# Attention keys in chunks of 128, 128, 128 and 64 in place of four chunks of 112

## The chip, the cores and the metric

The program runs on one core of a Trainium2 chip. The metric is the device time of one execution in microseconds (us); lower is better. Beside the timed runs one execution was recorded by the hardware profiler, and all lines of a profile below are from such an execution.

## What is computed

An attention block over 8 batches of 12 heads, with 448 positions and 64 values per head, followed by a two-layer block. All data is float32, only the two weight matrices arrive as float64.

```python
# q, k, v: (8, 12, 448, 64)
rmsnorm(x, g) = x / sqrt(mean(x * x, axis=-1) + 1e-6) * g
scores = (1 / 8) * rmsnorm(q, g_q) @ rmsnorm(k, g_k).T
attn   = exp(scores - max) / (sum(exp(scores - max)) + 1e-9)
o      = attn @ v                      # (8, 12, 448, 64)
x      = o.transpose(0, 2, 1, 3).reshape(3584, 768)
h      = x @ w_in                      # (3584, 2048)
out    = (h - tanh(h)) @ w_out         # (3584, 768)
```

## The kernel before

The work is cut into 48 steps: 8 batches times 6 pairs of heads. A step `s` has these parts, each a function that the diff touches:

- `load` fetches q, k and v of the pair. A tile holds 112 partitions with 4 positions each (`CP` = 112, `NCH` = 4): position 4p+c is chunk c of partition p. q and v come in one DMA each, k in one per head. All go through the queue of SyncE (SP), which also carries the weights (`weight_load`, `ring_load`) and the output (`store`), in the order in which the program writes them.
- `squares` (ScalarE) and `norm` (VectorE, then GpSimd for the power -0.5) give the reciprocal root mean squares `rr`; `norm_q` scales q by them. k is not scaled: its factor enters as the scale of the exponential.
- `turn` transposes the four chunks of k and of q on TensorE and copies them out as `kT` and `qT`: the two heads lie on rows 0 to 63 and 64 to 127, the 448 positions on columns.
- `scores(s, half)`: for two of the four chunks of keys, and for both heads, one product of 64 rows (the head's values) by 112 columns (the chunk's keys) with all 448 queries moving. Two such products, one per head, stand on the two row halves of TensorE. ScalarE then takes the exponential into `p`, keys on partitions.
- `add` (VectorE, from step 10 on) sums the four chunks of `p` into `sum`, `totals` multiplies that sum (or, before step 10, the four chunks themselves) by ones, 32 columns wide, four products side by side on column quarters, and takes the reciprocal `rs`.
- `values`: for each chunk four products of 112 rows by 32 columns with 448 queries moving, side by side on the four column quarters of TensorE, accumulated over the chunks in one bank of PSUM. `divide` multiplies by `rs` into `xT`; GpSimd builds three combinations from those (`tt`).

The two layers of the second block are done batch by batch with a seven-product scheme on half matrices (`products`: 128 x 128 weights, 224 columns moving, tile names `mm<-xT,w_f`, `mm<-gT,w_f`, `mm<-tt,w_f`, `mm<-tg,w_f`, line L510). From batch 1 on their weights are fetched through a ring of six slots, five products ahead. In batch 0 they are built on the way from the float64 words by ScalarE, VectorE and GpSimd.

The order of instructions is written out by hand. `first_slot` runs for steps -3 to 5, while there is nothing of the second block to do. `slot(s)` runs for steps 6 to 47: it places the parts of steps s to s+4 around four calls of `run(gap)`, each of which puts a fixed share of the second block's products of the batch before on TensorE. What is left of them at the end follows in `run(1e9)`. TensorE takes its instructions in this order, so a part that becomes cheaper there brings all that follows forward.

PSUM has eight banks: five are handed out in turn by `sc_bank`, three by `mm_bank`. Who takes a bank waits until its last user's reader is done.

Every float32 product is two instructions of TensorE (two passes), each a weight load (PEld) and a matmul (PE).

Of the kernel before, what the change touches and what calls it, by code (L numbers as in the profile page):

```python
# [91 lines left out]

def bounded_path(tc, ctx, q, k, v, moe_w_in, moe_w_out, out, g_col, ident, ones, neg_half):

# [33 lines left out]
    BL = 32  # L128
    assert HS * 2 == S and HC * 2 == CD and SETS * 4 == CF and HC * P == HALF and S % BL == 0

# [23 lines left out]
    def load(s, names):  # L154
        b, hp = steps[s]
        for name in names:
            src = {"q": q, "k": k, "v": v}[name]
            bufs = 3 if name == "v" else 2
            pair = src[b, 2 * hp : 2 * hp + 2].rearrange("h (p c) d -> p h c d", c=NCH)
            if name == "k":  # L160
                t = nat.tile([CP, NCH, 2, D], F32, name="k_nat", bufs=bufs)
                for h in range(2):
                    nc.sync.dma_start(out=t[:, :, h, :], in_=pair[:, h])
            else:
                t = nat.tile([CP, 2, NCH, D], F32, name=f"{name}_nat", bufs=bufs)
                nc.sync.dma_start(
                    out=t.rearrange("p h c d -> p h (c d)"), in_=pair.rearrange("p h c d -> p h (c d)")
                )
            loaded[name, s] = t
# [174 lines left out]
    def squares(s):  # L344
        n = nat.tile([CP, NCH, 2, D], F32, name="n", bufs=1)
        sq = nat.tile([CP, 2 * NCH, D], F32, name="sq", bufs=1), n.rearrange("p c h d -> p (c h) d")
        normed[s] = sq, n
        for i, name in ((1, "q"), (0, "k")):
            nc.scalar.activation(sq[i], loaded[name, s].rearrange("p a b d -> p (a b) d"), AF.Square)

    def norm(s):

        sq, n = normed[s]
        rr = small.tile([CP, 2, 2 * NCH], F32, name="rr", bufs=3)
        for group in ((1,), (0,)) if s < NP else ((0, 1),):
            for i in group:
                nc.vector.reduce_sum(rr[:, i], sq[i], axis=AX.X)  # L357
            r = rr[:, group[0] : group[-1] + 1].rearrange("p i r -> p (i r)")
            nc.vector.tensor_scalar(out=r, in0=r, scalar1=1.0 / D, scalar2=1e-6, op0=ALU.mult, op1=ALU.add)  # L359
            nc.gpsimd.tensor_tensor(out=r, in0=r, in1=neg_half[:, : r.shape[1]], op=ALU.pow)  # L360
        normed[s] = rr, n

    def norm_q(s):
        rr, n = normed[s]
        t = loaded.pop(("q", s))
        nc.vector.tensor_tensor(  # L366
            out=n.rearrange("p c h d -> p h c d"), in0=t,
            in1=rr[:, 1].rearrange("p (h c) -> p h c", h=2)[:, :, :, None].to_broadcast([CP, 2, NCH, D]),
            op=ALU.mult,
        )  # L370

    def turn(s, tk, tq):

        rr, n = normed.pop(s)
        kn = loaded.pop(("k", s))
        for c in range(NCH):
            nc.tensor.transpose(tk[:, c * CP : (c + 1) * CP], kn[:, c].rearrange("p h d -> p (h d)"), ident[:CP, :CP])  # L377
        kT = qkp.tile([P, S], F32, name="kT")
        nc.scalar.mul(kT, tk[:, :S], g_col)
        for c in range(NCH):  # L380
            nc.tensor.transpose(  # L381
                tq[:, c * CP : (c + 1) * CP], n[:, c].rearrange("p h d -> p (h d)"), ident[:CP, :CP]
            )
        qT = qkp.tile([P, S], F32, name="qT")
        nc.scalar.copy(out=qT, in_=tq[:, :S])
        turned[s] = rr, kT, qT
# [3 lines left out]

    def scores(s, half):

        rr, kT, qT = turned[s]
        p = probs[s, half] = pp.tile([CP, 2, NCH // 2, S], F32, name="p")
        for i in range(NCH // 2):
            c = half * (NCH // 2) + i
            tiles = []
            for h in range(2):
                r = slice(h * D, (h + 1) * D)
                sc = sc_bank()  # L400
                nc.tensor.matmul(  # L401
                    sc[:CP, :S], lhsT=kT[r, c * CP : (c + 1) * CP], rhs=qT[r, :], start=True, stop=True
                )
                tiles.append(sc)
            for h in range(2):
                nc.scalar.activation(  # L406
                    p[:, h, i, :], tiles[h][:CP, :S], AF.Exp, scale=rr[:, 0, 2 * c + h : 2 * c + h + 1]
                )

    def add(s):  # L410

        if s <= NP + NP // 2:
            sums[s] = []
            return
        t = sp.tile([CP, 2, S], F32, name="sum")
        sums[s] = [t]
        parts = [probs[s, c // 2][:, :, c % 2, :] for c in range(NCH)]
        nc.vector.tensor_tensor(out=t, in0=parts[0], in1=parts[1], op=ALU.add)  # L418
        for part in parts[2:]:
            nc.vector.tensor_tensor(out=t, in0=t, in1=part, op=ALU.add)  # L420

    def values(s, av):
        v_nat = loaded.pop(("v", s))
        for c in range(NCH):
            p = probs[s, c // 2]
            for m in range(2):
                for h in range(2):
                    r = (2 * m + h) * BL
                    nc.tensor.matmul(  # L429
                        av[r : r + BL, :S], lhsT=v_nat[:, h, c, m * BL : (m + 1) * BL], rhs=p[:, h, c % 2, :],  # L430
                        start=(c == 0), stop=(c == NCH - 1),
                    )
        return av

    def totals(s, dn):

        t = sums.pop(s)
        parts = t if t else [probs[s, c // 2][:, :, c % 2, :] for c in range(NCH)]
        for i, p in enumerate(parts):
            for n in range(2):  # L440
                for h in range(2):
                    r = (2 * n + h) * BL
                    nc.tensor.matmul(  # L443
                        dn[r : r + BL, :HS], lhsT=ones[:CP, :BL], rhs=p[:, h, n * HS : (n + 1) * HS],
                        start=(i == 0), stop=(i == len(parts) - 1),
                    )
# [3 lines left out]
    def divide(s, av):  # L450
# [3 lines left out]
        for n in range(2):  # L454
            for m in range(2):
                nc.vector.tensor_tensor(  # L456
                    out=x[m * D : (m + 1) * D, n * HS : (n + 1) * HS],
                    in0=av[m * D : (m + 1) * D, n * HS : (n + 1) * HS], in1=rs[n * D : (n + 1) * D], op=ALU.mult,
                )
        del probs[s, 0], probs[s, 1]  # L460
        if hp < HC:
# [257 lines left out]
    def first_slot(s):  # L719

        if has(s + 1):
            scores(s + 1, 0)
        if has(s + 2):
            turn(s + 2, mm_bank(), sc_bank())
        if s > -3:
            load(s + 4, "kq")
        squares(s + 3)
# [5 lines left out]
        if has(s + 1):  # L733
            scores(s + 1, 1)
            add(s + 1)
        av = values(s, mm_bank()) if has(s) else None
        norm_q(s + 3)
# [5 lines left out]
    def slot(s):  # L743
# [3 lines left out]
        if has(s + 1):  # L747
            scores(s + 1, 0)
        if has(s + 2):
            load(s + 2, "v")  # L750
# [5 lines left out]
        if has(s + 4):  # L756
            load(s + 4, "kq")
        run(gap)
        if s >= 2 * NP:
            totals(s, sc_bank())  # L760
        divide(s, values(s, sc_bank()))
        if has(s + 1):
            scores(s + 1, 1)
            add(s + 1)
# [6 lines left out]

    load(0, "kq")
    load(1, "kq")
    weight_load(0)
# [11 lines left out]
def general_path(tc, ctx, q, k, v, moe_w_in, moe_w_out, out, g_col, ident, neg_half):  # L786
# [67 lines left out]
    def prep(s):  # L854

        for name in ("k", "q"):
# [9 lines left out]
            )  # L866
            nc.gpsimd.tensor_tensor(out=rr, in0=rr, in1=neg_half[:, : 2 * NCH], op=ALU.pow)
            nc.vector.tensor_tensor(
# [145 lines left out]
def kernel(  # L1014
# [22 lines left out]
    consts = ctx.enter_context(tc.tile_pool(name="consts", bufs=1))  # L1037
    grow = consts.tile([1, 2, D], F32, name="grow")
    nc.scalar.dma_start(out=grow[:, 0, :], in_=g_q[None, :])
    nc.scalar.dma_start(out=grow[:, 1, :], in_=g_k[None, :])  # L1040
    gcol = consts.tile([P, 2], F32, name="gcol")
    for base in (0, D):
        nc.scalar.dma_start(out=gcol[base : base + D, 0:1], in_=g_q[:, None])
        nc.scalar.dma_start(out=gcol[base : base + D, 1:2], in_=g_k[:, None])
    prod = consts.tile([1, D], F32, name="prod")
    nc.vector.tensor_tensor(out=prod, in0=grow[:, 0, :], in1=grow[:, 1, :], op=ALU.mult)
    nc.vector.tensor_tensor(out=prod, in0=prod, in1=prod, op=ALU.mult)
    most = consts.tile([1, 1], F32, name="most")
    nc.vector.tensor_reduce(out=most, in_=prod, op=ALU.max, axis=AX.X)
    flag = consts.tile([1, 1], I32, name="flag")  # L1050
    nc.vector.tensor_scalar(
# [9 lines left out]
    nc.vector.memset(ones, 1.0)  # L1061
    neg_half = consts.tile([CP, 4 * NCH], F32, name="neg_half")
    nc.vector.memset(neg_half, -0.5)
    bounded = nc.values_load(flag[0:1, 0:1])

    with tc.If(bounded) as cmp:
        with ExitStack() as arm, tc.manual_schedule():
            bounded_path(tc, arm, q, k, v, moe_w_in, moe_w_out, out, g_col, ident, ones, neg_half)
    with cmp.Else():
# [32 lines left out]
```

## Time and profile before

| | |
|---|---|
| time of four runs | 1471.97 to 1474.83 us, median 1474.04 us |
| the profiled execution | 1471.86 us; span of its instructions 1470.1 us; granted TensorE clock 0.996 |
| busy, share of the span | PE 98%, PEld 78%, VectorE (DVE) 55%, ScalarE (ACT) 32%, GpSimd (POOL) 35% |
| DMA engines, mean share | 57.6% for the queue with all data |
| PE busy, 0 to 80 us | 60.75 us of 80 |
| PE busy, 330 to 1330 us | 999.26 us of 1000 |

How to read the lines: a group has the code line, the engine, the operation, the names of output and inputs, the tile's shape (rows*columns of weights, then partitions x elements that move), the count, the busy time and the mean nanoseconds of one, and behind the bar the time that the engine stood idle before them. In a timeline the first number is the start in us from the span's start, the second how long the merged row lasts; a row of PE ends with the drain of its last matmul, so the start of the next row tells the pace better than the length does. `xN` is the number of merged instructions, and in brackets stands the idle time before the row.

### The profile page before, as it was taken

The page shows a single profiled execution, that of the slowest core. Times are in us where ns is not written, and L with a number is a line of the kernel's source. Part 1 is how long each engine was busy: PE and PEld are TensorE (multiplying, and loading weights), DVE is VectorE, ACT ScalarE, POOL GpSimd, SP SyncE. Part 2 cuts the span into 40 slices and gives each one's busy share as a digit, 9 for nine tenths or more (in the row PEclk, how much of TensorE's full clock was granted, in tenths as well). Part 3 has the DMA queues.
Part 4 walks back from the last instruction along what each step waited for, and adds up shares of the span by engine and source line. Part 5 has one row for each costly group of instructions (what it writes and reads, how often), then busy time and mean ns, then how long its engine had stood idle before and what let it go on. Part 6 is the DMA issues. An engine that isn't in the chain of part 4 may idle for free.

```text
span 1470.1 us, 22159 instructions
## 1 busy us (share of the span) xinstructions
PE 1437.3 (98%) x8544; PEld 1146.7 (78%) x8544; DVE 806.7 (55%) x1162; ACT 468.4 (32%) x850; POOL 510.2 (35%) x336
## 2 busy tenths in 40 slices
PE   6889999999999999999999999999999999999997
PEld 2357744578887888788878887888788878889997
DVE  3889987756434653456445554545554366433322
ACT  6755544223222332133322332223322233201100
POOL 4556565233421343224423233322342134312310
PEclk9999999999999999999999999999999999999999
DMA  9759788954465454644454545555545654455563
GB/s 184 154 156 235 247 241 221 261 181 138 135 182 172 139 184 130 184 140 153 155 181 135 167 135 185 146 137 170 167 148 142 182 162 138 146 163 158 186 191 98
DMA packets 244998, 247.33 MB, mean 168 GB/s; under 512 B 143380, under 2 KB 187156, under 8 KB 244884
## 3 DMA queue, kind: packets, MB, share of 16 engines
q1 hardware_dynamic: 244560, 245.82, 57.6%
q8 instruction: 70, 1.15, 0.3%
q14 instruction: 44, 0.36, 0.1%
q10 hardware_dynamic: 324, 0.00, 0.0%
HBM read 212.34 MB, written 33.42 MB: 167 GB/s over the span
## 4 chain that ended last, share of the span: by engine, by line
PE 88%; DVE 7%; DMA 2%; issue 1%; SPq 1%; ACT 1%; POOL 1%; ACTq 0%; DVEq 0%; POOLq 0%
PE mm L510 62%; PE sc L401 9%; PE sc L429 8%; PE mm L675 4%; PE sc L443 2%; PE sc L381 1%; DMA q_nat<-in_q_dram 1%; PE sc L377 1%; DVE rr L357 1%; DVE sum L420 1%; DVE xT L456 1%; DMA w_raw<-in_moe_w_out_dram 1%; PE mm L429 1%; DVE w_out L275 1%; DVE sum L418 0%
## 5 line engine op out<-in xcount | busy, mean ns | idle before, releaser
L406 ACT ACTIVATE p<-sc,rr 112x448 f32<-112x448 f32 x384 | 212.2, 638 | 466.6 <-PE sc L401 454.6
L510 PE MATMUL mm<-xT,w_f 128*128 128x224 f32 x1392 | 279.4, 355 | 0.9 <-DVE s L576 0.6
L510 PEld LDWEIGHTS mm<-xT,w_f 128*128 128x128 f32 x1392 | 259.8, 190 | 20.3 <-issue 11.3
L510 PEld LDWEIGHTS mm<-gT,w_f 128*128 128x128 f32 x1344 | 251.4, 190 | 23.4 <-issue 22.7
L510 PE MATMUL mm<-gT,w_f 128*128 128x224 f32 x1344 | 267.7, 355 | 0.0
L360 POOL TENSOR_TENSOR rr<-rr,neg_half 112x16 f32<-112x16 f32 (+1 forms) x54 | 146.2, 2711 | 318.2 <-DVE rr L359 311.4
L510 PE MATMUL mm<-tt,w_f 128*128 128x224 f32 x1044 | 211.2, 354 | 0.0
L510 PEld LDWEIGHTS mm<-tt,w_f 128*128 128x128 f32 x1044 | 196.1, 190 | 8.0 <-issue 8.0
L510 PE MATMUL mm<-tg,w_f 128*128 128x224 f32 x1008 | 200.4, 353 | 0.0
L510 PEld LDWEIGHTS mm<-tg,w_f 128*128 128x128 f32 x1008 | 189.5, 190 | 0.0
L401 PE MATMUL sc<-qT,kT 64*112 64x448 f32 x768 | 175.3, 570 | 1.8 <-ACT p L406 1.2
L547 POOL TENSOR_TENSOR gT<-s,th 128x448 f32<-128x448 f32 x96 | 119.5, 1254 | 150.1 <-ACT th L546 149.5
L470 POOL TENSOR_TENSOR tt<-xT,tt 128x224 f32<-128x224 f32 x23 | 32.5, 1412 | 346.7 <-DVE xT L456 346.7
L401 PEld LDWEIGHTS sc<-qT,kT 64*112 64x112 f32 x768 | 63.5, 176 | 92.0 <-issue 78.9
L429 PE MATMUL sc<-p,v_nat 112*32 112x448 f32 x1344 | 134.1, 539 | 0.0
L420 DVE TENSOR_TENSOR sum<-sum,p 112x896 f32<-112x896 f32 x76 | 93.9, 1235 | 7.9
L429 PEld LDWEIGHTS sc<-p,v_nat 112*32 112x32 f32 x1344 | 43.1, 110 | 69.0 <-issue 64.1
L456 DVE TENSOR_TENSOR xT<-sc,rs 64x224 f32<-64x224 f32 x168 | 65.2, 388 | 57.7 <-PE sc L429 53.9
L546 ACT ACTIVATE th<-s 128x448 f32<-128x448 f32 x96 | 55.2, 578 | 119.0 <-DVE s L576 67.5
L366 DVE TENSOR_TENSOR n<-q_nat,rr 112x512 f32<-112x512 f32 x48 | 53.3, 1110 | 69.8 <-POOL rr L360 69.8
L448 DVE RECIPROCAL rs<-sc 128x224 f32<-128x224 f32 x42 | 65.4, 1558 | 39.4 <-PE sc L443 39.3
L629 DVE TENSOR_TENSOR s<-mm,s 128x224 f32<-128x224 f32 x21 | 8.2, 392 | 131.8 <-PE mm L510 131.8
(97 smaller groups left out, 1384.1 us busy)
## 6 DMA issues: line engine op xcount, KB each, us to landing
w_f<-w_in SPq DMA_DIRECT2D x196, 384.0 KB, 3.7
w_f<-w_out SPq DMA_DIRECT2D x147, 512.0 KB, 4.3
w_raw<-in_moe_w_out_dram SPq DMA_DIRECT2D x16, 768.0 KB, 5.3
k_nat<-in_k_dram SPq DMA_DIRECT2D x96, 112.0 KB, 3.5
q_nat<-in_q_dram SPq DMA_DIRECT2D x48, 224.0 KB, 4.4
v_nat<-in_v_dram SPq DMA_DIRECT2D x48, 224.0 KB, 4.6
out_dram<-th SPq DMA_DIRECT2D x192, 56.0 KB, 1.9
w_in<-w_out SPq DMA_DIRECT2D x21, 384.0 KB, 6.8
```

The lines of the kernel that those rows point to most:

```text
L360: nc.gpsimd.tensor_tensor(out=r, in0=r, in1=neg_half[:, : r.shape[1]], op=ALU.pow)
L366: nc.vector.tensor_tensor(out=n.rearrange("p c h d -> p h c d"), in0=t, in1=rr[:, 1].rearrange("p (h c) -> p h c", h=2)[:, :, :, None].to_ ...
L401: nc.tensor.matmul(sc[:CP, :S], lhsT=kT[r, c * CP : (c + 1) * CP], rhs=qT[r, :], start=True, stop=True)
L406: nc.scalar.activation(p[:, h, i, :], tiles[h][:CP, :S], AF.Exp, scale=rr[:, 0, 2 * c + h : 2 * c + h + 1])
L420: nc.vector.tensor_tensor(out=t, in0=t, in1=part, op=ALU.add)
L429: nc.tensor.matmul(av[r : r + BL, :S], lhsT=v_nat[:, h, c, m * BL : (m + 1) * BL], rhs=p[:, h, c % 2, :], start=(c == 0), stop=(c == NCH - 1),
L448: nc.vector.reciprocal(rs, dn[:, :HS])
L456: nc.vector.tensor_tensor(out=x[m * D : (m + 1) * D, n * HS : (n + 1) * HS], in0=av[m * D : (m + 1) * D, n * HS : (n + 1) * HS], in1=rs[n ...
L510: nc.tensor.matmul(bank[:, f * HS : (f + 1) * HS], lhsT=w[:, c * width + f, :], rhs=moving[p](c), start=(first and f == 0 and c == 0), sto ...
L546: nc.scalar.activation(th, h, AF.Tanh, bias=0.0, scale=1.0)
L547: eng.tensor_tensor(out=g[:, rows, cols], in0=h, in1=th, op=ALU.subtract)
L675: nc.tensor.matmul(bank[:, :S], lhsT=w_out_row(f, n // HC)[:, n % HC * P : (n % HC + 1) * P], rhs=g[:, f, :], start=(f == 0), stop=(f == C ...
```

## The change

The keys of a step go in three chunks of 128 and one of 64. A chunk of 128 holds positions 3p+c of the first 384; the last one holds positions 384 to 447. k and v of the last chunk are loaded twice, onto partitions 0 to 63 and 64 to 127, so k and v take two more DMAs each per step. q is issued ahead of k.

`turn` transposes k with 128 rows, so the last chunk's 64 keys come out twice; 448 of the 512 columns are copied. `scores` is called per chunk. For the chunks of 128 a product is 64 rows by 128 columns with 448 queries; for the last chunk there are four products of 64 rows by 64 columns with 224 queries each, on the four quarters of TensorE: row half by head, column half by half of the queries. So `p` of the last chunk has the first 224 queries on partitions 0 to 63 and the others on 64 to 127.

`values` works on 224 queries at a time in two banks. The last chunk goes first, in `last_values`: eight products of 64 rows by 32 columns with 224 queries, two row halves by four column quarters. Then follow, for each half of the queries, three chunks of 128 rows by 32 columns.

In `slot` the order of one turn changes: chunks 0 and 1 at its start (as before); behind the second `run(gap)` the last chunk's scores of step s+1, the last chunk's values of step s, the totals, the other values, and then the scores of chunk 2 (before: totals, values, scores of chunks 2 and 3). `norm` treats q and k apart in every step (before: in the first six alone), so there are two smaller powers on GpSimd in place of one.

```diff
@@ load
-            pair = src[b, 2 * hp : 2 * hp + 2].rearrange("h (p c) d -> p h c d", c=NCH)
-            if name == "k":
-                t = nat.tile([CP, NCH, 2, D], F32, name="k_nat", bufs=bufs)
-                for h in range(2):
-                    nc.sync.dma_start(out=t[:, :, h, :], in_=pair[:, h])
...
+                full, rest = pair[:, :K0].rearrange("h (p c) d -> h p c d", c=KF), pair[:, K0:]
+                if name == "v":
+                    t = nat.tile([P, 2, NCH, D], F32, name="v_nat", bufs=bufs)
+                    last = t[:, :, KF]
+                    nc.sync.dma_start(
+                        out=t[:, :, :KF].rearrange("p h c d -> p h (c d)"), in_=full.rearrange("h p c d -> p h (c d)")
+                    )
+                else:
+                    t = nat.tile([P, NCH, 2, D], F32, name="k_nat", bufs=bufs)
+                    last = t[:, KF]
+                    for h in range(2):
+                        nc.sync.dma_start(out=t[:, :KF, h], in_=full[h])
+                for r in range(2):
+                    nc.sync.dma_start(out=last[r * KR : (r + 1) * KR], in_=rest.rearrange("h p d -> p h d"))
@@ norm
-        for group in ((1,), (0,)) if s < NP else ((0, 1),):
...
+        for i, rows in ((1, CP), (0, P)):
+            r = rr[:rows, i]
+            nc.vector.reduce_sum(r, sq[i], axis=AX.X)
@@ turn
-            nc.tensor.transpose(tk[:, c * CP : (c + 1) * CP], kn[:, c].rearrange("p h d -> p (h d)"), ident[:CP, :CP])
+            nc.tensor.transpose(tk[:, c * P : (c + 1) * P], kn[:, c].rearrange("p h d -> p (h d)"), ident)
@@ scores
+        halves, keys, n = (1, P, S) if c < KF else (2, KR, HS)
+        name, bufs = ("p", 2) if c < 2 else ("p_full", 1) if c < KF else ("p_last", 2)
...
+        for i in range(halves):
             for h in range(2):
                 r = slice(h * D, (h + 1) * D)
                 nc.tensor.matmul(
-                    sc[:CP, :S], lhsT=kT[r, c * CP : (c + 1) * CP], rhs=qT[r, :], start=True, stop=True
+                    tiles[h][i * keys : (i + 1) * keys, :n], lhsT=kT[r, c * P : c * P + keys],
+                    rhs=qT[r, i * n : (i + 1) * n], start=True, stop=True,
                 )
@@ add
+        nc.vector.tensor_tensor(out=t, in0=p[0], in1=p[1], op=ALU.add)
+        nc.vector.tensor_tensor(out=t, in0=t, in1=p[2], op=ALU.add)
+        for n in range(2):
+            part = t[n * KR : (n + 1) * KR, :, n * HS : (n + 1) * HS]
+            nc.vector.tensor_tensor(out=part, in0=part, in1=last[n * KR : (n + 1) * KR], op=ALU.add)
@@ new function
+    def last_values(s, av):
+        v_nat, p = loaded["v", s], probs[s, KF]
+        for n in range(2):
+            keys = slice(n * KR, (n + 1) * KR)
+            for m in range(2):
+                for h in range(2):
+                    r = (2 * m + h) * BL
+                    nc.tensor.matmul(
+                        av[n][r : r + BL, :HS], lhsT=v_nat[keys, h, KF, m * BL : (m + 1) * BL],
+                        rhs=p[keys, h, 0], start=True, stop=False,
+                    )
@@ values
-        for c in range(NCH):
...
-                        av[r : r + BL, :S], lhsT=v_nat[:, h, c, m * BL : (m + 1) * BL], rhs=p[:, h, c % 2, :],
-                        start=(c == 0), stop=(c == NCH - 1),
+        for n in range(2):
+            for c in range(KF):
...
+                            av[n][r : r + BL, :HS], lhsT=v_nat[:, h, c, m * BL : (m + 1) * BL],
+                            rhs=p[c][:, h, n * HS : (n + 1) * HS], start=False, stop=(c == KF - 1),
@@ first_slot
-            load(s + 4, "kq")
+            load(s + 4, "qk")
...
-            scores(s + 1, 1)
+            scores(s + 1, KF)
+        if has(s):
+            av = [mm_bank() for _ in range(2)]
+            last_values(s, av)
+            values(s, av)
+        if has(s + 1):
+            scores(s + 1, 2)
             add(s + 1)
-        av = values(s, mm_bank()) if has(s) else None
@@ slot
+        if has(s + 1):
+            scores(s + 1, KF)
+        dn = sc_bank() if s >= 2 * NP else None
+        av = [sc_bank() for _ in range(2)]
+        last_values(s, av)
         if s >= 2 * NP:
-            totals(s, sc_bank())
-        divide(s, values(s, sc_bank()))
+            totals(s, dn)
+        divide(s, values(s, av))
         if has(s + 1):
-            scores(s + 1, 1)
+            scores(s + 1, 2)
             add(s + 1)
```

Before step 10 `totals` takes the last chunk with `half_ones`, ones on one half of the partitions and zeros on the other, so it still issues sixteen products. `divide` reads the two banks. The pools for `p` hold as much as before.

## The prediction

> **What bounds the kernel now.** I read the busy shares first, then the windows, then one turn of `slot` in the timeline.
>
> ```profile
> PE 1437.3 (98%) x8544; PEld 1146.7 (78%) x8544; DVE 806.7 (55%) x1162; ACT 468.4 (32%) x850; POOL 510.2 (35%) x336
> 0.00:80.00 80.00, 60.75 (x484) 26.41 (x484) 51.04 (x85) 55.22 (x97) 40.47 (x29) 0.98 0.85 176
> 330.00:1330.00 1000.00, 999.26 (x5998) 826.89 (x5991) 512.31 (x744) 285.79 (x541) 319.33 (x217) 1.00 0.52 155
> ```
>
> From about 120 us on, TensorE has no gaps: 999.26 us of 1000 in the long window, with VectorE at 51% and the DMA engines at 0.52. A microsecond less of TensorE work in `slot` is a microsecond less of time, unless something new makes it wait. Only the first 80 us (`first_slot`) are different. A busy row does not say how fast TensorE goes, so the starts in one turn come next (PE, then the weight loads):
>
> ```profile
> 825.22 0.35 PE L510 MATMUL mm<-xT,w_f 128*128 128x224 f32 x1
> 825.51 0.59 PE L443 MATMUL sc<-sum,ones 112*32 112x224 f32 x8
> 825.91 3.19 PE L429 MATMUL sc<-p,v_nat 112*32 112x448 f32 x32
> 829.03 1.76 PE L401 MATMUL sc<-qT,kT 64*112 64x448 f32 x8
> 830.72 0.46 PE L510 MATMUL mm<-xT,w_f 128*128 128x224 f32 x1
> ...
> 826.29 0.13 PEld L429 LDWEIGHTS sc<-p,v_nat 112*32 112x32 f32 x4 [0.25 <-issue]
> 826.66 0.13 PEld L429 LDWEIGHTS sc<-p,v_nat 112*32 112x32 f32 x4 [0.25 <-issue]
> ...
> 829.03 0.27 PEld L401 LDWEIGHTS sc<-qT,kT 64*112 64x112 f32 x4 [0.73 <-issue]
> 829.50 0.18 PEld L401 LDWEIGHTS sc<-qT,kT 64*112 64x112 f32 x2 [0.20 <-issue]
> 829.87 0.18 PEld L401 LDWEIGHTS sc<-qT,kT 64*112 64x112 f32 x2 [0.20 <-issue]
> 830.72 0.30 PEld L510 LDWEIGHTS mm<-xT,w_f 128*128 128x128 f32 x2 [0.67 <-issue]
> ```
>
> Weight loads come in fours (`values`) or twos (`scores`), and a group of 448 columns advances every 0.376 us (826.29, 826.66), whether it holds four products or two. `values` is 8 such groups, 825.91 to 829.03 = 3.12 us; half a step's scores are 4 groups, 829.03 to 830.72 = 1.69 us. What goes beyond 8 x 0.376 = 3.01 and 4 x 0.376 = 1.50 is the price of changing the tile's shape. It has two parts. The last group lasts longer: the last values group starts near 828.54, the scores 0.49 later, 0.11 too long; from the last scores group (830.25) to L510 it is 0.47, 0.10 too long; L510's own passes are 0.19 apart, and from its last (825.22) to the totals it is 0.29, 0.10 too long. And the first group's weights are not loaded ahead: 0.47 to the second scores group, 0.09 too long with 112 columns of weights; 0.30 to L510's second pass, 0.11 too long with 128; 0.02 too long for the totals' 32 (their second pass starts at 825.72). So a change of shape costs 0.12 us into 32 columns, 0.18 to 0.20 into the scores and 0.20 into L510.
>
> **The change part by part**, for one turn of `slot`.
>
> *Work removed.* Scores: 8 groups of 448 become 6 of 448 and 2 of 224 (four quarters at once, two passes). A group of 224 advances every 0.19 (totals, below), so 3.01 becomes 2.63: -0.37. Values: 8 groups of 448 become 2 of 224 (eight products at once, two passes) and 12 of 224: 3.01 becomes 2.65, -0.36. Together -0.74.
>
> That 224 columns cost half of 448 is shown by the early totals, 8 groups of four in a row:
>
> ```profile
> 36.35 1.72 PE L443 MATMUL mm<-p,ones 112*32 112x224 f32 x32
> 38.00 0.63 PE L401 MATMUL sc<-qT,kT 64*112 64x448 f32 x2
> ```
>
> 1.65 us less 0.13 for the two ends' changes of shape, over 8, is 0.19. This row shows no charge per instruction on products that run side by side. A page speaks against that: the Trainium skill, "TensorEngine Tiling (Array Packing)", Instruction Overhead, gives every matmul some 60 cycles of overhead and warns against cutting a dimension that is already small. By that, an estimate from the page with the 2.4 GHz of "TensorE: Matmul & The Clock Gate", the 36 matmuls that a turn gains would take 36 x 25 ns = 0.9 us, and the change would lose some 0.5 us a turn. I go by the row.
>
> *Changes of shape added.* Before: into scores, L510, 32 columns, scores, L510. After: into scores, L510, quarters, eighths, 32 columns of 128 rows, scores, L510. The change from L510 into 32 columns (0.12) goes; three come in. No row has quarters or eighths. I take 0.10 of drain plus the exposed weights in proportion to their columns: 0.15 into quarters (64 columns), 0.14 into eighths, 0.13 into the full chunks. Bounds: 0.12 to 0.20 each (the trace's cheapest and dearest), and nothing for quarters to eighths if a split of columns alone is free. Net +0.30, between +0.12 and +0.48. The same page, Key Properties, says that a change of tiling mode drains the engine and a change of tile does not; the two parts above are how that looks here.
>
> *Wider chunks.* Weights of 128 columns in place of 112 add 0.016 at two entries, 0.03. k's transposes move 128 columns in place of 112: in the timeline four of them take 0.39 (819.33 to 819.72), so 0.39 x 16/112 = 0.06.
>
> Sum per turn: -0.74 + 0.30 + 0.03 + 0.06 = -0.35 us, between -0.17 and -0.53. There are 42 turns (steps 6 to 47): -14.7 us, between -7 and -22.
>
> *Other engines in `slot`*, at nothing on the path. ScalarE: six exponentials of 638 ns and two of half the length for eight of 638: less. VectorE: in `add` one sum of 1235 ns becomes two of half its columns on half the partitions (0.4 to 0.65 us each, L456 takes 388 ns for 224), and `norm` gets one more 0.2 us instruction; cover is 49% idle time, and without cover it would be 0.3 us a turn. GpSimd: two powers of 1659 ns for one of 3012, at 32% busy. Banks: a turn takes 13 of the five in place of 12; each is free by some microseconds (the last scores take those of the quarters, whose exponentials have the 3 us of the values to end). Nothing on TensorE is given a wait for a result of the same turn. If the quarters' exponentials were late, the scores of chunk 2 would wait for their banks.
>
> *SP.* Four more issues a turn. k takes 0.61 us each (1.24 for two), v 0.45, so some 2.2 us more of queue time, past which the ring's loads are moved. From their landing in the trace to the first product of theirs at L510 there are 3.9 us and more outside of the entry into batch 1 (0.7 and 1.0 us at 285 and 295 us); cover in `slot`, and at most 2 us once. k and v grow from 1344 to 1760 packets a step with q; at 0.52 DMA share I cost that at nothing, and at 1 us in the first 80 us.
>
> *`first_slot`.* Here q's arrival leads the chain, and the issue order in the timeline shows why:
>
> ```profile
> 4.09 1.36 SPq L163 DMA_DIRECT2D k_nat<-in_k_dram  x2
> 5.50 0.61 SPq L166 DMA_DIRECT2D q_nat<-in_q_dram  x1
> ...
> 35.62 1.64 DVE L456 TENSOR_TENSOR xT<-mm,rs 64x224 f32<-64x224 f32 x4
> ```
>
> and in the chain of waits (start, length):
>
> ```profile
> 5.50 3.21 DMA q_nat<-in_q_dram
> 24.87 6.38 DMA q_nat<-in_q_dram
> 44.58 5.49 DMA q_nat<-in_q_dram
> 65.24 5.30 DMA w_raw<-in_moe_w_in_dram
> ```
>
> The chain has q's DMA three times (5.50, 24.87, 44.58), each behind two of k's issues (1.3 us): up to -4 us with q ahead. Against it: the raw weights' DMA is on the chain once (65.24) and now stands behind four more issues, +1 to +2.4; and `first_slot` takes four of the three `mm` banks a turn in place of three, so `totals` needs the bank that the `divide` before it reads. At 36.35 it began while that divide ran until 37.26: +0.9 a turn, up to five turns. VectorE, with 51 us of 80, would hide the first norms. I take +1, between -4 and +7.
>
> Whole: the profiled execution's own time (span 1470.1 and 1.8 around it) 1471.9 - 14.7 + 1 = 1458.2. That execution lies 2.2 us under the median of the four runs, 1474.0, so the forecast is 1460.4, rounded to 1460.5.
>
> **Rivals.** (A) The eighths run in more than two groups, or the changes of shape are dear. The eight products lie behind one another in the program, each with its two passes; if the second row half starts one pass late, 0.19 is lost and the gain is 0.16 a turn, 6.7 us: with +1, 1468. The same comes from the dearest changes. (B) One of quarters and eighths does not run side by side: 4 groups in place of 2, +0.38; net +0.03 a turn, 1476 with the early loss. (C) Slower: row and column split together are not run side by side at all. Every row of before splits either rows (scores, two at once) or columns (values, four at once), so nothing there excludes it. Quarters would go two by two and eighths four by four, 2 x 0.38 = +0.76 a turn, net +0.41, 42 turns: +17, with the early +1 1492. The turning point is 0.35 us a turn lost. For side by side speaks that each kind of split alone does so in every turn. The skill's "TensorE: Matmul & The Clock Gate", Part 3, reports sixteen 32 x 32 tiles at 10.6 times the speed of one, which no run here shows. (D) The change does not do what it says, because the time it takes from TensorE comes back as waits where weights are built (80 to 330 us: VectorE 206 us of 250 busy, DMA share 0.76): six turns of 0.35, 2 us, within the range.
>
> **How the numbers follow.** The forecast, with its own range of 1452 to 1468: 0.65 (D is in it). A 0.15, B 0.08, C 0.12. Of 0.2%, about what a measurement of this kernel can tell from no change (2.9 us): the forecast and A are faster, 0.80; B is the same, 0.08; C slower, 0.12. The range of 8 in 10 goes from the lowest sum (-22) at 1452 to B's 1476: what lies above is C.
>
> **What would show it.** `values` of 8 + 24 products: the first 16 matmuls `64*32` within 0.38 us plus entry, the next 48 at 0.19 a group, the whole (with its entries) 2.9 against 3.12 us; the last scores' eight `64*64` matmuls within 0.5 us. The sum of PE busy down by about 14 us, and 999 of 1000 still busy in the middle. Wrong if `64*64` or `64*32` records start in rows of more than two groups, if PE gets idle gaps before `p_last` or `p_full`, or if ring loads land behind their products.

## The result and the profile after

The changed kernel takes 1474.98 us (median of 40 runs, 1471.4 to 1481.0) against 1472.43 us before (62 runs): the ratio is 1.0018, with a 95% interval of 1.0014 to 1.0023. It is slower by some 2.6 us, where 13.5 us less were forecast. Its profiled execution has a span of 1474.2 us, against 1470.1.

The page (first line) and the windows of the changed kernel, with the columns of before:

```profile
PE 1434.4 (97%) x10272; PEld 1186.8 (81%) x10272; DVE 810.1 (55%) x1245; ACT 454.7 (31%) x850; POOL 508.5 (34%) x378
0.00:80.00 80.00, 62.37 (x692) 33.49 (x696) 54.19 (x97) 55.84 (x102) 42.85 (x33) 0.99 0.81 176
80.00:330.00 250.00, 239.23 (x1553) 161.84 (x1546) 198.20 (x269) 105.15 (x174) 122.36 (x75) 0.96 0.75 215
330.00:1330.00 1000.00, 996.47 (x7314) 855.46 (x7313) 520.22 (x814) 280.07 (x547) 317.80 (x249) 1.00 0.54 160
```

The second window of the kernel before was this (the first number behind POOL's is the granted clock of TensorE):

```profile
80.00:330.00 250.00, 244.88 (x1368) 161.33 (x1372) 205.82 (x269) 114.09 (x187) 126.48 (x71) 0.99 0.76 220
```

This window is where most of it went wrong: TensorE is busy for 239.23 of 250 us there (244.88 before) and its granted clock fell from 0.99 to 0.96. In the long window TensorE is idle for 3.5 us, 2.8 more than before.

One turn of `slot` in the timeline of the changed kernel shows that the work itself did what was forecast (L417 is `scores`, L452 the last chunk's values, L485 the totals, L464 the other values; `p_last` holds the exponentials of the last chunk, `p_full` those of chunk 2):

```profile
833.01 0.61 PE L417 MATMUL sc<-qT,kT 64*64 64x224 f32 x8
833.55 0.61 PE L452 MATMUL sc<-p_last,v_nat 64*32 64x224 f32 x16
834.09 0.58 PE L485 MATMUL sc<-sum,ones 128*32 128x224 f32 x8
834.50 0.94 PE L464 MATMUL sc<-p,v_nat 128*32 128x224 f32 x16
835.25 0.56 PE L464 MATMUL sc<-p_full,v_nat 128*32 128x224 f32 x8
...
836.88 1.02 PE L417 MATMUL sc<-qT,kT 64*128 64x448 f32 x4
837.83 3.29 PE L553 MATMUL mm<-xT,w_f 128*128 128x224 f32 x16
```

By the starts: the quarters take 0.54 us, the eighths 0.54, the totals 0.41, the other values 2.38 (834.50 to 836.88), chunk 2's scores 0.95. Together 4.82 us stand where 5.21 stood (825.51 to 830.72). That is 0.39 less; the wider scores and transposes of the turn take 0.06 of it back. The eighths do run side by side: sixteen matmuls in two groups.

To see where it went, I laid the start of each step's q transposes in the two traces beside each other (after less before, in us):

| step | 0 | 2 | 5 | 8 | 9 | 10 | 11 | 12 | 13 | 15 | 18 | 20 | 27 | 39 | 47 |
|---|---|---|---|---|---|---|---|---|---|---|---|---|---|---|---|
| difference | -0.6 | 1.6 | 1.1 | -3.3 | 1.2 | 1.0 | 7.5 | 6.8 | 11.1 | 11.3 | 10.6 | 9.9 | 8.9 | 6.6 | 5.0 |

Four things are in it. Up to step 8 the new kernel gains 3.3 us. Between steps 8 and 15 it loses 14.6 in three jumps of 4.5, 6.5 and 4.3 and a smaller one. Where nothing disturbs it, each turn gains 0.33 (18 to 20). And in each batch of six turns some 0.8 us go, 0.6 of them in one turn, so that a batch gains 1.2 and not 2.0.

The waits of TensorE name the jumps. The changed kernel (who waited for whom: us in total, times, longest; L498 is `divide`, L422 the exponential, L619 a read of a product's bank by VectorE):

```profile
PE sc L417 <- DVE xT L498: 7.7, 2, 5.1
PE mm L553 <- DVE s L619: 4.6, 6, 1.1
PE sc L417 <- ACT p_last L422: 3.5, 3, 1.9
```

Before, the lines of the same statements were the first two here, and none of the scores waited for `divide`. The third is a wait of the kernel before that the changed one does not have:

```profile
PE sc L401 <- ACT p L406: 1.2, 2, 0.9
PE mm L510 <- DVE s L576: 0.6, 4, 0.2
PE mm L510 <- DVE s L568: 1.5, 1, 1.5
```

The longest of them in the timeline (rows in order of time, other rows left out):

```profile
169.54 2.22 DVE L78 TENSOR_SCALAR w_out<-w_out 128x768 f32<-128x768 f32 x1
...
172.89 1.02 PE L417 MATMUL sc<-qT,kT 64*128 64x448 f32 x2
...
174.62 1.93 DVE L78 TENSOR_SCALAR w_out<-w_out 128x768 f32<-128x768 f32 x1
175.89 0.91 ACT L71 ACTIVATE w_out<-w_raw 128x768 f32<-128x768 f32 x1 [5.25 <-DMA w_raw<-in_moe_w_out_dram]
177.18 0.96 DVE L82 SCALAR_TENSOR_TENSOR w_out<-w_raw,w_out 128x768 int32<-128x768 int32 x1
177.49 0.76 ACT L422 ACTIVATE p_last<-sc,rr 128x224 f32<-128x224 f32 x2
178.05 1.64 DVE L498 TENSOR_TENSOR xT<-sc,rs 64x224 f32<-64x224 f32 x4
...
179.00 1.83 PE L417 MATMUL sc<-qT,kT 64*128 64x448 f32 x2 [5.09 <-DVE xT L498]
```

Chunk 2's scores for the first head start at 172.89, those for the second at 179.00. In the built program the second head's scores lie in the bank of the first half of the values of the same turn, so they wait for `divide`: they start behind the second of its four instructions. VectorE had next to no pause here. It was busy for 6.83 of the 7 us from 172 to 179, mostly with the rounding of weights (L78, L79, L82) whose words had landed by 168.9, and `divide` stood behind that in its queue. ScalarE did wait, 5.25 us for the next raw weight's DMA, and the last chunk's exponentials stood behind it (177.49); a wait for those is the jump between steps 12 and 13, where the second head's scores lie in a bank of the last chunk's. In the kernel before, the same `divide` was as late (177.13, with the values finished near 171.5), and nothing on TensorE asked for it in that turn.

A wait also costs what follows it, as the windows of the changed kernel show:

```profile
172.00:179.00 7.00, 1.91 (x25) 0.71 (x15) 6.83 (x9) 2.88 (x5) 3.22 (x3) 0.88 0.64 129
179.00:182.00 3.00, 3.00 (x5) 1.64 (x6) 2.28 (x6) 0.63 (x1) 2.52 (x2) 0.50 1.01 384
182.00:186.00 4.00, 4.00 (x17) 3.78 (x17) 0.62 (x1) 0.00 (x0) 1.92 (x2) 0.73 1.04 417
```

TensorE has half its clock when it goes on, and until 184.1 us. From chunk 2's first scores (172.89) to the first `mm<-xT,w_out` behind them (183.91) 11.0 us pass; in the second experiment below, where nothing waits there, the same work takes 2.57 (167.30 to 169.87). Of the 8.4 us lost, 6.1 are the delay of the second head's scores and 2.3 the slower clock. The jump is 6.5 and not 8.4 because the kernel before had the wait of 1.5 us for VectorE (L568) in this turn, and the smaller work gives 0.3.

### The profile page after: what moved, and what is told of

The parts are those of the page before. It is cut to its first block, busy times and chain, and to the rows that moved or that the text cites. A ratio compares the mean times of both kernels' runs of the same rounds, so it can differ in the third digit from the quotient of the medians.

```text
span 1474.2 us, 26066 instructions
## 1 busy us (share of the span) xinstructions
PE 1434.4 (97%) x10272; PEld 1186.8 (81%) x10272; DVE 810.1 (55%) x1245; ACT 454.7 (31%) x850; POOL 508.5 (34%) x378
## 4 chain that ended last, share of the span: by engine, by line
PE 88%; DVE 6%; DMA 2%; SPq 1%; ACT 1%; issue 1%; POOL 0%; ACTq 0%; DVEq 0%; POOLq 0%
PE mm L553 64%; PE sc L417 9%; PE sc L464 6%; PE mm L718 3%; PE sc L485 2%; PE sc L452 1%; PE sc L390 1%; PE sc L394 1%; DVE rs L490 1%; DMA w_raw<-in_moe_w_out_dram 1%; DVE w_out L79 1%; DVE xT L498 1%; DVE w_out L78 1%; DVE w_out L82 1%; DVE rr L371 1%
## 5 line engine op out<-in xcount | busy, mean ns | idle before, releaser
L373 POOL TENSOR_TENSOR rr<-rr,neg_half 112x8 f32<-112x8 f32 x96 | 157.9, 1666 | 313.8 <-DVE rr L372 311.6
L417 PE MATMUL sc<-qT,kT 64*128 64x448 f32 (+1 forms) x960 | 172.8, 498 | 12.6 <-DVE xT L498 7.7
L422 ACT ACTIVATE p<-sc,rr 128x448 f32<-128x448 f32 x192 | 106.0, 638 | 200.3 <-PE sc L417 200.3
L590 POOL TENSOR_TENSOR gT<-s,th 128x448 f32<-128x448 f32 x96 | 112.8, 1182 | 153.7 <-ACT th L589 153.6
L417 PEld LDWEIGHTS sc<-qT,kT 64*128 64x128 f32 (+1 forms) x960 | 62.5, 166 | 82.1 <-issue 70.1
L490 DVE RECIPROCAL rs<-sc 128x224 f32<-128x224 f32 x42 | 65.4, 1557 | 77.6 <-PE sc L485 77.5
L422 ACT ACTIVATE p_full<-sc,rr 128x448 f32<-128x448 f32 x96 | 56.0, 631 | 150.3 <-PE sc L417 150.3
L464 PE MATMUL sc<-p,v_nat 128*32 128x224 f32 x1344 | 79.1, 353 | 0.0
L718 PE MATMUL mm<-gT,w_out 128*128 128x448 f32 x192 | 76.0, 552 | 0.0
L422 ACT ACTIVATE p_last<-sc,rr 128x224 f32<-128x224 f32 x96 | 37.8, 447 | 114.9 <-PE sc L417 114.9
L498 DVE TENSOR_TENSOR xT<-sc,rs 64x224 f32<-64x224 f32 x168 | 65.3, 389 | 9.7 <-PE sc L464 2.3
```

The costliest lines, as they stand in the source:

```text
L373: nc.gpsimd.tensor_tensor(out=r, in0=r, in1=neg_half[:rows], op=ALU.pow)
L417: nc.tensor.matmul(tiles[h][i * keys : (i + 1) * keys, :n], lhsT=kT[r, c * P : c * P + keys], rhs=qT[r, i * n : (i + 1) * n], start=True, ...
L422: nc.scalar.activation(p[:, h, c if c < 2 else 0, :], tiles[h][:, :n], AF.Exp, scale=rr[:, 0, 2 * c + h : 2 * c + h + 1])
L464: nc.tensor.matmul(av[n][r : r + BL, :HS], lhsT=v_nat[:, h, c, m * BL : (m + 1) * BL], rhs=p[c][:, h, n * HS : (n + 1) * HS], start=False, ...
L490: nc.vector.reciprocal(rs, dn[:, :HS])
L498: nc.vector.tensor_tensor(out=x[m * D : (m + 1) * D, n * HS : (n + 1) * HS], in0=av[n][m * D : (m + 1) * D, :HS], in1=rs[n * D : (n + 1) * ...
```

## The experiments

Two theories for the 14 us: **banks** (chunk 2's scores wait for a bank whose reader is late) and **weights** (the weights themselves come later, because k and v take more DMAs, and TensorE would wait somewhere anyway). Each timed kernel has its own runs of before beside it, 1472.3 or 1472.4 us; ratios are to those.

**Chunk 2 a gap later** (`e1_chunk2_later`), steps 6 to 11 alone:

```diff
-        if has(s + 1):
+        if s >= 2 * NP and has(s + 1):
             scores(s + 1, 2)
             add(s + 1)
         if has(s + 3):
             norm(s + 3)
         run(gap)
+        if s < 2 * NP:
+            scores(s + 1, 2)
+            add(s + 1)
```

> In steps 6 to 11 alone, the scores of chunk 2 stand behind the third run(gap) in place of straight behind the values. Theory (banks): the 14 us lost between 99 and 320 us are TensorE waiting at the scores of chunk 2 for the PSUM bank of the values just made, whose reader divide is late in VectorE's queue, or of the last chunk's scores, whose exponentials are late in ScalarE's, and for the slower clock behind such a wait. Moved by a gap of some 7 us the wait is over before it is asked for: three waits of 2.8, 5.3 and 2.1 us vanish with their tails, -14 us, less 0.2 us of one more change of shape in each of six turns: 1462. Rival (weights): the weights of batch 0 themselves come later because of four more DMAs a turn, and TensorE would wait for them elsewhere: 1473 to 1476.

Measured: 1462.61 us, ratio 0.994 (0.9926 to 0.9953). In the turn above the second head's scores still take the bank of the values, but a gap later, and no wait for `divide` is left among TensorE's waits. Step 15 lies 2.2 us ahead of before, where the changed kernel is 11.3 behind. The weights theory falls: k and v have the same DMAs here.

**The quarters a gap earlier** (`e2_quarters_earlier`), steps 6 to 11 alone:

```diff
             turn(s + 2, sc_bank(), sc_bank())
+        if s < 2 * NP:
+            scores(s + 1, KF)
...
-        if has(s + 1):
+        if s >= 2 * NP and has(s + 1):
             scores(s + 1, KF)
```

> In steps 6 to 11 alone, the last chunk's scores stand behind the transposes, a gap earlier; the scores of chunk 2 stay straight behind the values. Theory (banks): it is one bank too many in one place that makes the wait (last chunk 2, values 2, chunk 2's scores 2, with five banks); with the last chunk's pair read out earlier, the scores of chunk 2 get its banks and wait for nothing: 1462 as with chunk 2 moved. Rival (order): scores straight behind the values wait for VectorE or ScalarE whatever bank they get, so 1473 to 1476 here and a gain only where chunk 2 is moved.

Measured: 1461.02 us, ratio 0.9926 (0.9912 to 0.9939). Chunk 2's scores stand where the change put them, straight behind the values, and go through at once. The timeline of this kernel, at the same turn:

```profile
167.30 1.02 PE L417 MATMUL sc<-qT,kT 64*128 64x448 f32 x4
168.25 1.78 PE L553 MATMUL mm<-tt,w_out 128*128 128x224 f32 x8
...
170.09 0.94 ACT L71 ACTIVATE w_out<-w_raw 128x768 f32<-128x768 f32 x1 [3.70 <-DMA w_raw<-in_moe_w_out_dram]
...
172.29 1.64 DVE L498 TENSOR_TENSOR xT<-sc,rs 64x224 f32<-64x224 f32 x4
```

`divide` runs at 172.29, 5 us behind the scores, and nobody on TensorE minds. So it is not the place behind the values that waits, but the count of banks that are wanted there at one time: two for the quarters, two for the values, two for chunk 2, with five to give. Before it was one for the values and four for the scores. In the window from 80 to 330 us the clock is back at 1.00. What is left of waits for `p_last` in the whole kernel is 1.6 us in two.

**k first** (`e3_k_first`), and the kernel before with **q first** (`e7_before_q_first`). The edit of the first is this, with the same in two more places; the second is its reverse:

```diff
-    load(0, "qk")
+    load(0, "kq")
...
-            load(s + 4, "qk")
+            load(s + 4, "kq")
```

> k is issued ahead of q again, the rest as changed. Theory: the 3.3 us gained up to step 8 come from q's earlier arrival, since q's DMA led the chain of the first 80 us: here 3 to 4 us more, 1478.5, with step 8's transposes some 3.5 us later. Rival: they come from less work on TensorE and ScalarE in the first nine turns (9 x 0.33 = 3 us), and the order costs nothing: 1475.

> The kernel before with nothing changed but q issued ahead of k. Theory (q's arrival leads the first 80 us): step 8's transposes 2 to 4 us earlier, and as TensorE is dense from 120 us on, the time down by as much unless the weights' waits take it back: 1469 to 1471. Rival (the early gain needs the smaller work too): within 1 us of 1472.3.

Measured: 1476.98 us, ratio 1.0036 (1.0022 to 1.005), so 2 us more than the changed kernel, between theory and rival. In its trace step 8 comes 3.1 us later (98.92 against 95.77). Not all of that need be q's DMA: the clock was at half from 36.0 to 42.8 us in this execution, which it was not in the changed kernel's. By step 13 nothing of the 3.1 us is left between these two traces (10.5 and 11.1 us behind before): the last of the three jumps is 1.7 us with k first, in place of 4.3.

In the kernel before, q first brings step 8 forward by 1.93 us and TensorE's last matmul by 2.0, but the time is 1471.81, ratio 0.9995 (0.9986 to 1.0004): not to be told from no change, as the rival had it, though not for the rival's reason. In that profile the outputs have landed 1.6 us earlier than before (1466.4 against 1468.0), yet the span ends 9.6 us behind the last matmul, against 7.7: SyncE, in its last waits, lets 1.8 us pass between two of them (1467.09 and 1468.90), and in no other profile here does it. Why is open. So q's order does lead the first 80 us and gives 2 to 3 us there. How much of it stays in the time was not settled: one edit showed 2 us, the other 0.6.

**k's half of `norm` later** (`e4_norm_k_later`), from step 12 on: its reduction, its scaling and its power stand behind `norm_q`, after the third gap. `norm_part` does one half of `norm`, and `k_part` keeps k's half for later; both are defined in `norm`, which is left out here.

```diff
...
             norm_q(s + 3)
+            if s + 3 in k_part:
+                norm_part(*k_part.pop(s + 3), 0, P)
         run(gap)
```

> From step 12 on, k's half of norm (two VectorE instructions, 0.9 us, and a power on GpSimd) stands behind the third run(gap). Theory: the 0.9 us that TensorE waits once a batch at L553 for DVE s L619 is VectorE's queue, 0.4 us longer in add and norm and started 0.3 us later against TensorE; 0.9 us out of it ends the wait: -0.75 us in each of 6 batches, 1470.5. Rival: the wait hangs on the product's place alone and VectorE's queue has nothing to do with it: 1475.

Measured: 1469.48 us, ratio 0.9978 (0.9969 to 0.9987), some 5.5 us under the changed kernel, a little more than the 4.5 expected. The long window of this kernel:

```profile
330.00:1330.00 1000.00, 1000.00 (x7341) 861.37 (x7340) 524.11 (x817) 279.88 (x547) 322.07 (x251) 1.00 0.54 160
```

No idle time at all: the wait once a batch was VectorE's queue, `add` and `norm` ahead of the read that frees a bank of the second block. From step 21 to 45 the lead grows by 2.2 us a batch, or 0.37 a turn.

**Both** (`e5_both`): the quarters earlier and k's half of `norm` later.

> The last chunk's scores a gap earlier in steps 6 to 11 and k's half of norm later from step 12 on, together. Theory: the two losses are apart in time and add up: 1461.0 - 0.75 x 7 = 1456. Rival: the second is partly the first's echo, 1459 to 1461.

Measured: 1455.58 us, ratio 0.9884 (0.9869 to 0.9899). It beats both kernels, by 16.8 us the one before. Its windows:

```profile
80.00:330.00 250.00, 246.69 (x1712) 168.97 (x1711) 206.51 (x284) 112.19 (x190) 125.76 (x77) 1.00 0.78 226
330.00:1330.00 1000.00, 1000.00 (x7281) 864.04 (x7280) 520.51 (x812) 275.40 (x538) 319.79 (x249) 1.00 0.54 161
```

## Why the prediction was wrong, step by step

- **Work and changes of shape: right.** -0.35 us a turn was forecast and 0.33 measured where nothing waits. The parts were as sized: 0.09 to 0.14 of drain and 0.02 to 0.05 of exposed weights at the new shapes (the second group of quarters starts 0.24 behind the first, the second of eighths 0.21, and without exposure it is 0.19), 0.109 for each of k's transposes. Rivals A to C fell: 64 x 64 and 64 x 32 products run side by side as rows or columns alone did. That the time came out near B's 1476 is chance, for B's reason did not occur. A charge for each of the added matmuls does not appear: a turn has 36 more of them and is 0.33 us shorter.
- **Banks: the step that failed.** It said that each bank "is free by some microseconds" and that "Nothing on TensorE is given a wait for a result of the same turn". The turn that the prediction shows is at 825 us, where ScalarE and VectorE are up to date; in the six turns of batch 0 they run up to 6 us behind because of the raw weights. The text even named a wait ("the scores of chunk 2 would wait for their banks") and gave it no price. It also put chunk 2's scores into the banks of the quarters; in the built program that is so in most turns, but in the first three of batch 0's six the second head's scores lie in a bank of the values just made. The waits cost 4.5, 6.5 and 4.3 us by the steps' starts, in three turns of six, with 1.7 to 3.3 us lost to halved clock in each. Experiments 1 and 2 each take it away, by 12.4 and 14.0 us.
- **Rival D: right place, wrong size.** It put the danger at 80 to 330 us, with VectorE 206 us of 250 busy, and priced it at 2 us, the gain that could be lost. A wait has no such limit.
- **VectorE's norms and sums: costed at nothing, 5.5 us in the time.** Cover was said to be 49% idle time. The idle time is an average; once a batch the read that frees a product's bank stood behind 5.3 us of `add` and `norm` (838.14 to 843.44) that were 4.9 before, and its cover there had been 0.2 us short already (the wait of 0.16 at 836.44 before). The fourth experiment takes it away.
- **SP: at nothing, right.** No product waits for a load of the ring; the one DMA among TensorE's waits is k's first, 8.1 us at the start against 7.8 before. The packets grew by 480 a step and not by the 416 that the text has, and nothing in the waits shows it.
- **First 80 us: +1 forecast, -3.3 measured at step 8.** q's earlier DMA is 2 to 3 us of it by the third experiment. The four `mm` banks cost 2.7 us in two waits, not of `totals` for the `divide` before it, as feared, but of k's transposes for the bank that the totals' reciprocal reads (PE mm L390 <- DVE rs L490).

## What to carry to other kernels

Before a saving on the busiest engine is written down, count the buffers that the new order wants at one time, and look at every stretch of the program where the engines that free them run late, not at one typical turn. An engine at 50% can still be late by microseconds where its queue holds a block of other work or a wait for a DMA; ask for each result how late it may be, and who asks for it now that did not before. When a change brings less than its own work says, lay the starts of the same step in both traces side by side: jumps are waits, a slope is work.

## What was not expected of the hardware

When TensorE stood idle for 5.1 us, its clock was granted at 0.50 from 177.3 us, still within the wait, to 184.1. Around the end of an idle stretch of 2.65 us it was so from 109.0 to 115.9, which is 6.8 us again, and behind one of 1.9 us from 249.0 to 252.4 (0.66 in the 5 us from 248 to 253). In the second experiment a wait of 1.8 us (176.34) left it at 1.00. So in these traces the length of the idle stretch alone does not tell how long the clock will be slow. Products of 64 rows by 32 columns went eight at a time, and their two passes 0.21 us apart, against 0.24 for four of 64 by 64. Each product's two passes follow one another in the built program, and yet all first passes start together: the eight of a group begin 7 ns apart, within 50 ns, and the second passes only then.
